# A gated product and its splits moved between two ticks, with tables, gates and small copies moved in their queues

## The chip, the cores and the metric

The kernel runs on one core of a Trainium2 chip. The core has several engines that each work through a queue of their own, in order: TensorE (PE, matrix products, results to PSUM banks), VectorE (DVE), ScalarE (ACT, functions from tables that have to be loaded), GpSimd (POOL), and SyncE (SP), which here issues the DMAs. Semaphores tie the queues together. The metric is the device time of one execution in microseconds (us); less is better.

## The reference

A block with 2048 tokens of width 576 takes two branches and mixes them by a gate for each token.

```
g = sigmoid((x * gate_w).sum(-1, keepdims=True))
a = _A_ref(x, A_wq, A_wk, A_wv, A_wo, A_beta)     # attention in 4 segments of 512, 32 heads of 18
b = _B_ref(x, B_w_gate, B_w_up, B_w_down)         # silu(x @ w_gate) * (x @ w_up) @ w_down, 576 -> 4608 -> 576
return g * a + (1 - g) * b
```

Branch a handles each segment with softmax attention inside it, and adds a linear memory `M` (with its normalizer `z`) of all segments before:

```
p = _softmax(logits, axis=-1)
a_dot = jnp.einsum("bhqk,bhkd->bhqd", p, vs)
...
a_mem = num / den
o = g * a_mem + (1.0 - g) * a_dot
...
pk = phi(ks)
M = M + jnp.einsum("bhld,bhle->bhde", pk, vs)
z = z + jnp.einsum("bhld->bhd", pk)
```

## The kernel before

The program is one long order of instructions, written out in Python. The order of the code is the order of each engine's queue. It has four stretches.

**Projections** (about 5 to 234 us). For each segment s of 512 tokens, ten chains of Q and K (`qk`, L449; n counts them) and then a loop of V steps (`v_step`, L475). Between the chains `upd_gen` (L496) updates the memory: it transposes `ph` tiles on PE (L513, L516), copies them out of PSUM into `kt` (512 columns by ACT at L514, 64 by DVE at L517), and multiplies them (L505). `mem_step` reads the memory (L550). Beside it all, inputs for the next stretch are made: sums on POOL (`rest_sum`, `first_sum`) and splits into a high half on ACT and a low one on DVE (`rest_split`, `first_split`). Tables by n say when: RSTEP (L661; a number j is a split, a negative one a sum), FSUM and FSPLIT (L729, L730).

**Half 0 and half 1 of the FFN** (to about 921 and 1631 us). The hidden width is cut into 36 slices, f = 0 to 35, and the tokens into two halves. For each half and f a block runs: seven products in the manner of Strassen (`seven`, L1421, j = 0 to 6) give the up and the gate values of two banks of 512 tokens. At the end ACT makes the silu `sg0` (L1540) and `sg1` (L1542), and DVE multiplies them by the up values: `sg0` from PSUM at L1548, after `seven(xx, 6)`, and `sg1` from SBUF at L1549. Each product is then split in fp16: high part `hh` on ACT (L1295), low part `hl` on DVE (L1298). `split_by(k, ...)` puts them on the list `due`, k ticks ahead; `lag` is the distance between the two.

Between the products a block has eight places named `tick()` (k = 0 to 7). Ticks 5 and 6 stand between `seven(y, 5)` and `seven(xx, 6)`, tick 7 behind it. Each tick runs what is due (weight preparation `w_make`, with L369 on POOL, L373 on ACT and L377 on DVE; splits; loads), and then, as `SHARE = (0, 0, 2, 2, 3, 3, 3, 3)` says, some of the **down groups**, with steps of attention between them (`att_gen`: scores L889 and L1002, exponentials on ACT L1006, maxima on DVE L907, probabilities by DVE L1102 and POOL L1106).

A down group multiplies three slices of `hh` and `hl` by the down weights `dw`: nine matmuls (L1162) into a bank, which DVE then adds to `ya` (L1171; L1169 for the first). `feed` (L1325) lists sixteen groups, eight token tiles by two column halves. They run in each block with q = f mod 3 = 0 and f > 0, for the three slices before it; groups 0 and 1 at tick 2, and so on to 7 to 9 at tick 5, 10 to 12 at tick 6 and 13 to 15 at tick 7. Two banks take turns, so that group n+2 waits for the eviction of group n.

The down weights of half 0 are split into three parts by `d_split` (L1139, L1140, L1142 or L1144). The gate of each token needs exponentials (`gates`, L1412 on). As silu and exponential have different tables on ACT, `exp_table` (L1418) runs a dummy exponential, so that the table is loaded at a chosen place.

**The break** after f = 35 of half 0 (about 899 to 921 us): the last sixteen down groups, ten beats in a row, without `seven` between them. The inputs of half 1's remainder products are split by `rest_second`, by a list `todo` with due times.

**The output** (1631 us to the end): the last down groups and the output projection.

Of the kernel before, what the change touches and what calls it, by code (L numbers as in the profile page):

```python
# [17 lines left out]
AF = mybir.ActivationFunctionType  # L18
OP = mybir.AluOpType
# [50 lines left out]
def gated_mix(ctx, tc, xT, xrest, wf, wfr, wfh, wd, wv, wo, beta, cmask, ident, bmask, out):  # L70
# [323 lines left out]
    with ExitStack() as st:  # L394
# [40 lines left out]
        def flush(keep=0):  # L435
            while len(late) > keep:
                z = late.pop(0)
                for d in z if isinstance(z, list) else [z]:
                    nc.sync.dma_start(*d)
# [56 lines left out]
        def upd_gen(s):  # L496
            acc = [pair_tile([P, 3, MW]), pair_tile([P, 2, MW])]
            Mo, Mn = Mm[s % 2], Mm[(s + 1) % 2]
            for i in range(5):
                if i:  # L500
                    for k in range(NT):
                        a, b = HR[k]
                        n = (b - a) * E
                        kk = P if k < 4 else 64
                        nc.tensor.matmul(acc[k // 3][:kk, k % 3, :n], kt[:, P * k:P * k + kk],  # L505
                                         vf[:, i - 1].rearrange("p h e -> p (h e)")[:, a * E:b * E],
                                         start=(i == 1 and k % 3 == 0), stop=(i == 4), skip_group_check=True)
                if i < 4:
                    kt = sp.tile([P, D], F32, name="kt", bufs=1)
                    c = slice(P * i, P * i + P)  # L510
                    ta = half_tile([P, 4, P])
                    for k in range(4):
                        nc.tensor.transpose(ta[:, k], phi[s, k, 1][:, c], idt)  # L513
                    nc.scalar.activation(kt[:, 0:512], ta.rearrange("p a b -> p (a b)"), AF.Copy)  # L514
                    tb = lone_tile([P, P])
                    nc.tensor.transpose(tb, phi[s, 4, 0][:, c], idt)  # L516
                    nc.vector.tensor_copy(kt[:, 512:576], tb[:, 64:128])  # L517
                yield
            for k in range(NT):
                n = (HR[k][1] - HR[k][0]) * E  # L520
                kk = P if k < 4 else 64
                t = acc[k // 3][:kk, k % 3, :n]
                if s == 0:
                    nc.vector.tensor_mul(Mn[:kk, k, :n], t, bm[:kk, k, :n])
                else:
                    tmp = sp.tile([P, MW], F32, name="mtmp")
                    nc.vector.tensor_mul(tmp[:kk, :n], t, bm[:kk, k, :n])
                    nc.gpsimd.tensor_add(Mn[:kk, k, :n], Mo[:kk, k, :n], tmp[:kk, :n])
            yield
# [128 lines left out]
            rest_16(XR[j], rr[((0, 0), (0, 0), (1, 1), (0, 1), (1, 0), (1, 1), (0, 1))[j]])  # L658

        XR = [None] * 7  # L660
        RSTEP = {2: (0, 3), 3: (5, -1), 4: (1, -4), 5: (4, -2), 6: (2,), 7: (-6,), 8: (6,)}  # L661
        rb, rs = {}, {}

        def b_load(i):
# [56 lines left out]
        def scan_load(t):  # L721
# [3 lines left out]
            if t in (21, 30):  # L725
                b_load(t // 30)

        blocks = {3: [(0, 0)], 4: [(0, 1)], 5: [(0, 2), (1, 0)], 6: [(1, 1)], 7: [(1, 2)]}
        FSUM = {3: [(1, 0), (4, 0)], 4: [(2, 0), (1, 1)], 6: [(4, 1), (2, 1)], 7: [(6, 0)], 8: [(6, 1)]}  # L729
        FSPLIT = {2: [(0, 0)], 3: [(5, 0), (0, 1)], 4: [(1, 0), (4, 0)], 5: [(5, 1), (2, 0)], 6: [(1, 1), (3, 0)],  # L730
                  7: [(3, 1), (4, 1)], 8: [(2, 1)]}
        for s in range(NSEG):
            upd = upd_gen(s - 1) if s else None
            casts = []
            for n, (m, u) in enumerate(chains):
                mid = []
                if s == 0:
                    for z in loads.get(n, []):
                        z()
                    if n + 3 < 9:  # L740
                        mid.append(lambda n=n: q_split(*chains[n + 3]))
                    if n in halves:
                        mid.append(lambda n=n: v_split(*halves[n]))
                if s == 1 and n < 3:
                    cast = masks(*((0, 3), (3, NT), (0, 0))[n])
                    casts.append(cast)
                if s == 1 and 3 <= n < 6:
                    mid.append(casts[n - 3])
                if (s, n) == (1, 7):
                    mid.append(betas)  # L750
                mid += scan_step(17 * s + n)
                if (s, n) == (1, 7):
                    mid.append(lambda: total(sx, 0, 20))
                if s == 2:
                    if n == 5:
                        mid.append(lambda: weigh(1, half_tile([P, 9])))
                    if n == 0:
                        rest_load()
                    for z in blocks.get(n, ()):
                        mid.append(lambda z=z: b_step(*z))  # L760
                    for j in RSTEP.get(n, ()):
                        mid.append(lambda j=j: rest_split(j) if j >= 0 else rest_sum(-j))
                if s == 3:
                    if n < 4:
                        first_load(n)
                    for j, z in FSPLIT.get(n, []):
                        if j in (0, 3, 5):
                            mid.append(lambda j=j, z=z: first_split(j, z))
                    for j, z in FSUM.get(n, []):
                        mid.append(lambda j=j, z=z: first_sum(j, z))  # L770
                    for j, z in FSPLIT.get(n, []):
                        if j in (1, 2, 4):
                            mid.append(lambda j=j, z=z: first_split(j, z))
                if s < 3:
                    for kt in ((0, 1), (2, 3), (4,))[n - 6] if s == 0 and n > 5 else (n - 4,) if s and n > 3 else ():
                        raws["x", kt] = x_load(s + 1, kt)
                qk(s, m, u, mid)
                flush(2)
                scan_load(17 * s + n)
                if upd is not None and n > 0:  # L780
                    next(upd, None)
# [16 lines left out]
            for n in range(8):  # L798
# [23 lines left out]
                else:  # L822
                    if n == 4:
                        wraw_of[1] = [w_load(1, u) for u in range(2)]
                    if n < 2:
                        first_split(6, n)
                    for k, t, v in ((0, rhs[0][96:], 0.0), (1, kst[0], -1.0), (3, kst[1], -1.0), (4, rhs[1][96:], 0.0)):
                        if n == k:
                            nc.gpsimd.memset(t, v)
# [13 lines left out]
    with ExitStack() as st:  # L843
# [479 lines left out]
                        c_open()  # L1323

        def feed(half, f):  # L1325
            return [(f // CH, i, hf, hs, ds, half) for i in range(8) for hf in range(2)]

        def x_second(new, z):
            r = {}
# [40 lines left out]
        def rest_second(rest):  # L1370
# [19 lines left out]
            def low(j):  # L1390
                t = rest[j][32:64]
                nc.vector.scalar_tensor_tensor(t, source(j)[32:64], sx[32:64], t, op0=OP.mult, op1=OP.subtract)

            todo = [(-1, load, 0), (0, high, 0), (0, high, 3), (1, low, 0), (1, low, 3), (4, load, 1), (11, high, 5),
                    (11, total, 1), (12, low, 5), (12, high, 1), (13, total, 4), (13, low, 1), (14, total, 2),
                    (14, high, 4), (15, low, 4), (15, total, 6), (16, high, 2), (16, low, 2), (17, high, 6), (18, low, 6)]
            return [(o, lambda fn=fn, j=j: fn(j)) for o, fn, j in todo]

        def glance(i, k):
# [12 lines left out]
        def gates():  # L1412
            nc.scalar.activation(gg, gl, AF.Exp, scale=-1.0)
            defer(2, lambda: nc.vector.tensor_scalar_add(gg, gg, 1.0))
            defer(3, lambda: nc.vector.reciprocal(gg, gg))
            defer(4, lambda: nc.vector.tensor_scalar(g1, gg, -1.0, 1.0, op0=OP.mult, op1=OP.add))

        def exp_table():  # L1418
            nc.scalar.activation(bg[:, 0:1], idt[:, 0:1], AF.Exp)
# [14 lines left out]
        for pos, (half, f) in enumerate(seq):  # L1434
# [49 lines left out]
            def tick():  # L1484
# [5 lines left out]
                if half == 0:  # L1490
# [6 lines left out]
                        d_scale(f // CH)  # L1497
                    if (f, k) == (2, 7) or (f > 2 and (q, k) == (1, 3)):
                        d_back(f // CH)
                    if f == 2 and k > 4 or f > 2 and (q, k) in ((1, 1), (1, 7), (2, 5 + int(f < FT - 1))):  # L1500
                        g = k - 5 if f == 2 else f - 1 if k == 1 else f
                        ds[half, g] = d_split(g, draw.pop(g))
                elif (q, k) in ((1, 0), (1, 2), (2, 1)):
                    g = f - 1 if k == 0 else f
# [12 lines left out]
            p5, sg0, sg1 = (row_tile() for _ in range(3))  # L1517
            seven(a, 0)
            nc.scalar.activation(xx, a, AF.Copy)
            if half == 0 and q == 0 and f:  # L1520
                exp_table()
                if f == CH:
                    gates()
            tick()
            seven(y, 1)
            nc.scalar.activation(p5, y, AF.Copy)
# [13 lines left out]
            nc.scalar.activation(sg0, sg0, AF.Silu, scale=iw[f // 4])  # L1540
            seven(y, 5, False)
            nc.scalar.activation(sg1, y, AF.Silu, scale=iw[f // 4])  # L1542
            if (half or q == 0) and not cps:
                exp_table()
            tick()
            tick()
            seven(xx, 6, False)
            nc.vector.scalar_tensor_tensor(sg0, xx, hk[f // 4], sg0, op0=OP.mult, op1=OP.mult)  # L1548
            nc.vector.scalar_tensor_tensor(sg1, p5, hk[f // 4], sg1, op0=OP.mult, op1=OP.mult)  # L1549
            split_by(2, hh[:, 0], hl[:, 0], sg0, int(q < CH - 1))  # L1550
            split_by(3, hh[:, 1], hl[:, 1], sg1)
            tick()
            assert not groups
            if f == FT - 1:
# [111 lines left out]
```

## Time and profile before

| | |
|---|---|
| three runs | 1721.46, 1718.13 and 1721.53 us, median 1721.46 |
| the profiled execution | 1718.78 us, of which the span from first to last instruction is 1717.1 |
| mean granted TensorE clock | 0.998 |
| projections | 0 to 234 us |
| half 0, break, half 1 | 234 to 899, 899 to 921, 921 to 1631 us |
| output | 1631 to 1717 us |

The profile gives for each engine its busy time, the chain of work that ended last, and groups of instructions by line, tile and form. `bank<-dw,hl` means that tile `bank` is written from `dw` and `hl`; `128x512 f16<-128x512 f32` are the shapes and types of output and input. Views of the trace give single instructions (start and duration in us), PE's waits by what ended them, and busy times in chosen windows. A matmul's row ends by a model of its pipeline, so rows of one engine may overlap a little.

### The profile page before, as it was taken

To read this page: it belongs to the slowest core of one execution; us is meant where nothing else is said; L and a number is where in the kernel's file an instruction comes from. 1 tells how busy PE (TensorE), PEld (TensorE's weight loads), DVE (VectorE), ACT (ScalarE), POOL (GpSimd) and SP (SyncE) were. 2 spreads that over 40 slices of the span, in tenths; PEclk is the share of its full clock that TensorE was granted. 3 is DMA by queue.
4 is the path that set the end of the run, shared out by engine and by line. 5 is a ranking of instruction groups with operands and counts; after the bars stand their busy time and mean duration, and the time that the engine had idled before them with its cause. 6 is when DMAs were issued, how large, how long until landed. Compare 5 with 4: busy or idle time off the path is not lost.

```text
span 1717.1 us, 35318 instructions
## 1 busy us (share of the span) xinstructions
PE 1679.5 (98%) x12269; PEld 1077.8 (63%) x12269; DVE 1353.8 (79%) x3295; ACT 1076.6 (63%) x1930; POOL 889.2 (52%) x1191
## 2 busy tenths in 40 slices
PE   9999999999999999999999999999999999999999
PEld 7898865556655665565555656556656656655577
DVE  6687676789888988898886878788878788776466
ACT  7666567777777777767774654665556566565411
POOL 3336562266667665665452665465546565554121
PEclk9999999999999999999999999999999999999999
DMA  8666675666776675446535486796696597574544
GB/s 282 218 232 222 214 260 208 208 200 177 231 223 208 168 244 192 154 121 195 169 123 164 114 192 158 163 219 136 147 215 166 121 221 167 140 163 125 156 157 145
DMA packets 349542, 314.25 MB, mean 183 GB/s; under 512 B 201268, under 2 KB 266548, under 8 KB 349364
## 3 DMA queue, kind: packets, MB, share of 16 engines
q1 hardware_dynamic: 349364, 312.00, 63.5%
q8 instruction: 96, 1.57, 0.4%
q14 instruction: 82, 0.67, 0.1%
HBM read 186.15 MB, written 99.55 MB: 166 GB/s over the span
## 4 chain that ended last, share of the span: by engine, by line
PE 73%; DVE 12%; ACT 7%; issue 3%; DMA 3%; POOL 1%; SPq 1%; DVEq 0%; ACTq 0%; POOLq 0%
PE bank L1426 31%; PE bank L1162 18%; PE bank L223 8%; PE bank L1429 5%; PE bank L889 3%; PE bank L1002 2%; DVE ya L1171 1%; PE bank L1030 1%; ACT L1540 1%; DVE junk L907 1%; PE bank L1032 1%; PE bank L964 1%; DVE p L1102 1%; ACT row L1540 1%; DMA rc<-rt 1%
## 5 line engine op out<-in xcount | busy, mean ns | idle before, releaser
L1162 PE MATMUL bank<-dw,hh 128*128 128x320 f16 (+1 forms) x2304 | 437.5, 286 | 13.3 <-DVE ya L1171 8.9
L1162 PE MATMUL bank<-dw,hl 128*128 128x320 f16 (+1 forms) x1152 | 330.1, 287 | 3.8 <-DVE hl L1298 3.2
L1106 POOL TENSOR_TENSOR p<-pe,p 128x512 f16<-128x512 f32 x220 | 271.9, 1236 | 75.3 <-DVE p L1102 50.6
L1162 PEld LDWEIGHTS <-hh 128*128 128x128 f16 x2304 | 225.3, 98 | 99.9 <-issue 18.1
L1006 ACT ACTIVATE pe<-bank 128x512 f32<-128x512 f32 x220 | 130.1, 592 | 183.6 <-PE bank L1002 167.5
L1171 DVE SCALAR_TENSOR_TENSOR ya<-bank,sc,ya 128x320 f32<-128x320 f32 x352 | 176.2, 511 | 55.0 <-PE bank L1162 53.3
L1429 PE MATMUL bank<-xr,rh 128*128 128x512 f16 x504 | 191.0, 379 | 0.0
L907 DVE CUSTOM_DVE_ANT_0 junk<-bank,cm 128x128 bf16<-128x128 f32 (+2 forms) x352 | 169.3, 481 | 13.7 <-PE bank L889 7.3
L1298 DVE SCALAR_TENSOR_TENSOR hl<-hh,row 128x512 f16<-128x512 f16 x144 | 129.7, 902 | 45.7 <-ACT hh L1295 44.8
L1014 POOL TENSOR_SCALAR_AFFINE_SELECT pe<-pe 128x256 f32<-128x256 f32 (+1 forms) x220 | 89.3, 406 | 144.9 <-ACT pe L1006 137.3
L1162 PEld LDWEIGHTS <-hl 128*128 128x128 f16 x1152 | 112.7, 98 | 34.3 <-DVE hl L1298 3.8
L889 PE MATMUL bank<-kst,qst 108*128 108x512 bf16 (+3 forms) x512 | 124.5, 299 | 3.6 <-ACT pe L1006 2.9
L1002 PE MATMUL bank<-qst,kst 111*128 111x512 bf16 (+3 forms) x352 | 103.2, 300 | 1.1 <-DVE acc L975 1.1
L1102 DVE CAST p<-pe 128x512 f16<-128x512 f32 x203 | 103.3, 510 | 0.0
L369 POOL TENSOR_TENSOR ws<-raw 128x256 f32<-128x256 f32 x72 | 65.6, 912 | 63.4 <-DMA raw<-in_wf_dram 32.2
L1538 DVE TENSOR_TENSOR row<-bank,row 128x512 f32<-128x512 f32 x72 | 49.6, 689 | 60.9 <-ACT bank L1537 60.8
L223 PE MATMUL bank<-xo,qhi 128*128 128x512 f32 x288 | 92.5, 401 | 1.3 <-ACT xo L132 0.7
L466 POOL TENSOR_TENSOR q<-qr,q 128x512 bf16<-128x512 f32 x36 | 47.8, 1329 | 84.8 <-ACT q L465 77.0
L1295 ACT ACTIVATE hh<-row 128x512 f16<-128x512 f32 x144 | 89.0, 618 | 3.7 <-DVE row L1548 3.0
L1533 ACT ACTIVATE row<-bank 128x512 f32<-128x512 f32 x72 | 42.9, 596 | 73.7 <-PE bank L1429 73.7
L1537 ACT ACTIVATE bank<-bank 128x512 f32<-128x512 f32 x72 | 41.9, 581 | 72.8 <-PE bank L1429 70.9
L1429 PEld LDWEIGHTS <-rh 128*128 128x128 f16 x504 | 49.3, 98 | 59.6 <-issue 0.2
(1102 smaller groups left out, 4213.9 us busy)
## 6 DMA issues: line engine op xcount, KB each, us to landing
xo<-in_wf_dram SPq DMA_DIRECT2D x65, 320.0 KB
raw<-in_wf_dram SPq DMA_DIRECT2D x72, 256.0 KB
dc<-dw SPq DMA_DIRECT2D x36, 432.0 KB
dw<-dc SPq DMA_DIRECT2D x36, 432.0 KB
rh<-rc SPq DMA_DIRECT2D x72, 168.0 KB
draw<-in_wd_dram SPq DMA_DIRECT2D x36, 288.0 KB
xo<-in_xT_dram SPq DMA_DIRECT2D x33, 256.0 KB
vd<-vps SPq DMA_DIRECT2D x8, 912.0 KB
```

The source lines that it names most:

```text
L223: nc.tensor.matmul(t, st[n], mv[n], start=(n == 0), stop=(n == 13))
L889: nc.tensor.matmul(t[:, c:c + w], qs[:KR, pr, P * i:P * i + P], ks[:KR, pr, 0:w], start=True, stop=True)
L907: nc.vector.tensor_tensor_reduce(junk.bitcast(BF)[:, :w], t[:, c:c + w], cm[:, L - w:L], 1.0, -3.0e38, OP.add, OP.max, m[:, k:k + 1])
L1002: nc.tensor.matmul(t[:, c:c + w], ks[:KR + 3, pr, P * j:P * j + P], qs[:KR + 3, pr, P * j:L], start=True, stop=True)
L1006: nc.scalar.activation(pe, t, AF.Exp, scale=SCALE)
L1102: nc.vector.tensor_copy(p1, pe)
L1106: nc.gpsimd.tensor_sub(p2, pe, p1)
L1162: nc.tensor.matmul(t, p, d[:, q, cs], start=(f == CH * c and n == 0), stop=(f == CH * c + CH - 1 and n == 2))
L1171: nc.vector.scalar_tensor_tensor(ya[:, i, cs], t, inv[c], ya[:, i, cs], op0=OP.mult, op1=OP.add)
L1298: nc.vector.scalar_tensor_tensor(lo, hi, -STEP, src, op0=OP.mult, op1=OP.add)
L1426: nc.tensor.matmul(t, w[:, p, z], x[z][:, q], start=first and n == 0, stop=False, skip_group_check=True)
L1429: nc.tensor.matmul(t, rem[:, RPOS[j]], XR[j], start=False, stop=True, skip_group_check=True)
```

## The change

- The 64-wide key copy of L517 is done by ACT.
- In segment 2 the last remainder sum is made one step earlier (n = 6), and its split behind chain (2, 8). In segment 3 what stood at n = 8 goes into the V loop.
- `exp_table` isn't called at f = 0, and at f = 3 only after `seven(y, 5)`, with `gates` behind it; from f = 6 on as before.
- The product of `sg1` (L1549) no longer stands behind that of `sg0`. In blocks with q = 0, other than the first of all, it stands between ticks 5 and 6, else between tick 6 and `seven(xx, 6)`.
- The splits change places: bank 1 (`sg1`) first, with the shorter lag, then bank 0. `feed` lists token tiles 4 to 7, which lie in bank 1, ahead of 0 to 3.
- The last down weight of half 0 is split at tick 2 in place of 5.
- The due times of `rest_second` from 11 on are two later.

```diff
-                    nc.vector.tensor_copy(kt[:, 512:576], tb[:, 64:128])
+                    nc.scalar.activation(kt[:, 512:576], tb[:, 64:128], AF.Copy)
...
-        RSTEP = {2: (0, 3), 3: (5, -1), 4: (1, -4), 5: (4, -2), 6: (2,), 7: (-6,), 8: (6,)}
+        RSTEP = {2: (0, 3), 3: (5, -1), 4: (1, -4), 5: (4, -2), 6: (2, -6)}
...
-        FSUM = {3: [(1, 0), (4, 0)], 4: [(2, 0), (1, 1)], 6: [(4, 1), (2, 1)], 7: [(6, 0)], 8: [(6, 1)]}
+        FSUM = {3: [(1, 0), (4, 0)], 4: [(2, 0), (1, 1)], 6: [(4, 1), (2, 1)], 7: [(6, 0)]}
...
-                  7: [(3, 1), (4, 1)], 8: [(2, 1)]}
+                  7: [(3, 1), (4, 1)]}
...
                 qk(s, m, u, mid)
+                if (s, n) == (2, 8):
+                    rest_split(6)
...
-                    if n < 2:
-                        first_split(6, n)
+                    if n == 0:
+                        first_split(2, 1)
+                        first_sum(6, 1)
+                    if 1 <= n < 3:
+                        first_split(6, n - 1)
...
         def feed(half, f):
-            return [(f // CH, i, hf, hs, ds, half) for i in range(8) for hf in range(2)]
+            return [(f // CH, i, hf, hs, ds, half) for i in (4, 5, 6, 7, 0, 1, 2, 3) for hf in range(2)]
...
-            todo = [(-1, load, 0), (0, high, 0), (0, high, 3), (1, low, 0), (1, low, 3), (4, load, 1), (11, high, 5),
+            todo = [(-1, load, 0), (0, high, 0), (0, high, 3), (1, low, 0), (1, low, 3), (4, load, 1), (13, high, 5),
...
-                    if f == 2 and k > 4 or f > 2 and (q, k) in ((1, 1), (1, 7), (2, 5 + int(f < FT - 1))):
-                        g = k - 5 if f == 2 else f - 1 if k == 1 else f
+                    if f == 2 and k > 4 or f > 2 and (q, k) in ((1, 1), (1, 7), (2, 6 if f < FT - 1 else 2)):
+                        g = k - 5 if f == 2 else f - 1 if (q, k) == (1, 1) else f
...
-            if half == 0 and q == 0 and f:
+            if half == 0 and q == 0 and f > CH:
                 exp_table()
-                if f == CH:
-                    gates()
...
-            if (half or q == 0) and not cps:
+            if (half or q == 0 and f) and not cps:
                 exp_table()
+                if half == 0 and f == CH:
+                    gates()
             tick()
+            if q == 0 and pos:
+                nc.vector.scalar_tensor_tensor(sg1, p5, hk[f // 4], sg1, op0=OP.mult, op1=OP.mult)
             tick()
+            if q or not pos:
+                nc.vector.scalar_tensor_tensor(sg1, p5, hk[f // 4], sg1, op0=OP.mult, op1=OP.mult)
             seven(xx, 6, False)
             nc.vector.scalar_tensor_tensor(sg0, xx, hk[f // 4], sg0, op0=OP.mult, op1=OP.mult)
-            nc.vector.scalar_tensor_tensor(sg1, p5, hk[f // 4], sg1, op0=OP.mult, op1=OP.mult)
-            split_by(2, hh[:, 0], hl[:, 0], sg0, int(q < CH - 1))
-            split_by(3, hh[:, 1], hl[:, 1], sg1)
+            split_by(2, hh[:, 1], hl[:, 1], sg1, int(q < CH - 1))
+            split_by(3, hh[:, 0], hl[:, 0], sg0)
             tick()
```

More of the change, by code (lines that the diff above doesn't have):

```diff
@@ L1392, in low @@
                 nc.vector.scalar_tensor_tensor(t, source(j)[32:64], sx[32:64], t, op0=OP.mult, op1=OP.subtract)
-            todo = [(-1, load, 0), (0, high, 0), (0, high, 3), (1, low, 0), (1, low, 3), (4, load, 1), (11, high, 5),
-                    (11, total, 1), (12, low, 5), (12, high, 1), (13, total, 4), (13, low, 1), (14, total, 2),
-                    (14, high, 4), (15, low, 4), (15, total, 6), (16, high, 2), (16, low, 2), (17, high, 6), (18, low, 6)]
+            todo = [(-1, load, 0), (0, high, 0), (0, high, 3), (1, low, 0), (1, low, 3), (4, load, 1), (13, high, 5),
+                    (13, total, 1), (14, low, 5), (14, high, 1), (15, total, 4), (15, low, 1), (16, total, 2),
+                    (16, high, 4), (17, low, 4), (17, total, 6), (18, high, 2), (18, low, 2), (19, high, 6), (20, low, 6)]
             return [(o, lambda fn=fn, j=j: fn(j)) for o, fn, j in todo]
```

## The prediction

> **What bounds the kernel now.** The page's first part, then its chain by engine, say that TensorE is the bound nearly everywhere.
>
> ```profile
> PE 1679.5 (98%) x12269; PEld 1077.8 (63%) x12269; DVE 1353.8 (79%) x3295; ACT 1076.6 (63%) x1930; POOL 889.2 (52%) x1191
> ```
>
> The change adds and removes no matmul. So only three things can move the end: the 37.6 us (1717.1 − 1679.5) in which PE stands still, the stretches in which its clock is lowered, and new waits. The list of PE's waits over the whole run (us in total, times, longest) says what the idle time hangs on:
>
> ```profile
> PE bank L1162 <- DVE ya L1171: 8.9, 18, 1.0
> PE bank L1162 <- DVE hl L1298: 3.2, 2, 2.1
> PE bank L505 <- DVE kt L517: 1.8, 2, 1.1
> PE bank L1426 <- ACT bank L1519: 1.7, 3, 0.6
> PE bank L550 <- DVE ph L468: 1.3, 1, 1.3
> PE bank L1162 <- DVE dw L1140: 1.1, 1, 1.1
> PE bank L1162 <- ACT hh L1295: 1.1, 2, 0.9
> PE bank L223 <- DVE r L486: 0.8, 1, 0.8
> PE bank L1162 <- DVE dw L1142: 0.6, 1, 0.6
> ```
>
> All but the first and the r row are waits that an edit aims at. The first, PE waiting for a PSUM bank that VectorE still evicts (`ya`), is the one that the change can lengthen. The table of windows shows the lowered clock (PEclk, third from the right), each time after a stretch in which PE was broken up:
>
> ```profile
> 273.00:276.60 3.60, 1.65 (x10) 0.71 (x9) 2.37 (x6) 3.26 (x8) 0.00 (x0) 1.00 0.90 304
> 277.10:280.60 3.50, 3.50 (x14) 1.73 (x12) 2.44 (x7) 1.41 (x3) 1.45 (x2) 0.53 1.03 393
> 898.90:903.90 5.00, 2.05 (x15) 1.16 (x13) 4.71 (x6) 2.80 (x6) 2.86 (x2) 1.00 0.13 47
> 905.10:908.60 3.50, 3.50 (x17) 2.30 (x16) 1.08 (x3) 0.00 (x0) 0.00 (x0) 0.52 0.94 284
> ```
>
> Half speed for 3.5 us costs about 1.7 us each time, 3.4 together.
>
> **The change part by part.** The timeline of PE gives each gap (start, duration, then idle time and releaser in brackets):
>
> ```profile
> 65.76 0.35 PE L505 MATMUL bank<-vf,kt 128*64 128x76 f32 x2 [1.06 <-DVE kt L517]
> 196.41 0.35 PE L505 MATMUL bank<-vf,kt 128*64 128x76 f32 x2 [0.72 <-DVE kt L517]
> 159.82 0.93 PE L550 MATMUL bank<-Mm,ph 128*128 128x152 f32 x6 [1.35 <-DVE ph L468]
> 248.53 1.46 PE L1426 MATMUL bank<-xo,wo__2849 128*128 128x512 f16 x6 [0.53 <-ACT bank L1519]
> 901.39 0.45 PE L1162 MATMUL bank<-dw,hh 128*128 128x320 f16 x2 [0.89 <-ACT hh L1295]
> 903.90 0.31 PE L1162 MATMUL bank<-dw,hl 128*128 128x320 f16 x1 [2.06 <-DVE hl L1298]
> 904.05 0.38 PE L1162 MATMUL bank<-dw,hh 128*128 128x256 f16 x2
> 1634.70 0.31 PE L1162 MATMUL bank<-dw,hl 128*128 128x320 f16 x1 [1.10 <-DVE hl L1298]
> ```
>
> A matmul's row is longer than its step in flow: 0.31 us at 903.90, but the next starts 0.15 later. So each gap loses some 0.16 more than its idle figure.
>
> *Key copies* (L517 from DVE to ACT, 12 times). Two gaps, 1.06 + 0.72 + 2 × 0.16 = 2.1. On ACT the copy follows L514 directly. No row shows a 64-wide one there; the 128x1 activation of L1419 takes 0.20 us (row below) and the 512-wide L514 takes 0.58, so it costs 0.20 to 0.58; I take 0.3, nearest the narrow one. ACT's timeline has L514 done well ahead of the first gap's end (start, duration):
>
> ```profile
> 62.76 0.58 ACT L514 ACTIVATE kt<-bank 128x512 f32<-128x512 f32 x1
> ```
>
> That is 63.34, over a microsecond ahead of PE's need, which hides the copy. Gain 2.0 (1.5 to 2.1).
>
> *Remainder sums*. In segment 2 the last sum moves a step earlier, where POOL is idle for 3.07 us:
>
> ```profile
> 150.72 1.39 POOL L466 TENSOR_TENSOR q<-qr,q 128x512 bf16<-128x512 f32 x1 [3.07 <-ACT q L465]
> ```
>
> So the long DVE subtraction which it stretched, and the split queued ahead of `ph`, leave the path. The gap is 1.35 + 0.16; the matmuls after it would wait about 0.4 for their own operand. Gain 1.1 (0.8 to 1.5). In segment 3 the r gap hangs on copies that aren't moved, and one more split stands at n=2: +0.1 (0 to 0.3).
>
> *Tables and gates*. Four table loads and two dummy exponentials go. Rows of ACT's timeline, and of its groups:
>
> ```profile
> 245.88 1.28 ACT L1419 ACT_TABLE_LOAD   x1
> 271.50 1.28 ACT L1419 ACT_TABLE_LOAD   x1
> L514 ACT ACTIVATE kt<-bank 128x512 f32<-128x512 f32 x12 | 6.9, 578 | 0.0
> L1419 ACT ACTIVATE bg<-idt 128x1 f32<-128x1 f32 x58 | 11.8, 203 | 0.6
> ```
>
> Most of ACT's 4 × 1.28 us is beside PE's work. On the path are the gap at 248.53 (0.53 + 0.16) and two smaller ones at 257.9 and 262.9, some 0.45 together: gain 1.15 (0.7 to 1.2). At f=3 the load and the two gate exponentials, 1.28 + 0.20 + 0.20, stand ahead of hh, and so of hl and the third weight's two splits, which are the dw waits of 1.1 and 0.6 in the list; with the two small waits beside them PE loses 2.45 there and, with everything on ACT 1.68 earlier, about 0.85 remains. Gain 1.6 (1.2 to 2.4). If that takes the lowered clock behind it away, 1.7 more (0 to 1.7).
>
> *Break after half 0*. The gaps at 901.39 and 903.90 lose 0.89 + 2.06 + 0.32 = 3.3. VectorE has six operations in a row there (4.71 us busy of 5.00), one of them this, ahead of the two hl that PE waits for (start, duration):
>
> ```profile
> 900.59 1.36 DVE L1549 SCALAR_TENSOR_TENSOR row<-row,sc 128x512 f32<-128x512 f32 x1
> ```
>
> The last weight's splits (0.8 and 1.4 us of DVE) move three ticks ahead and this product ahead of the last `seven`; bank 1, ready first, is then used first. PE needs the other bank only after eight groups. I leave 0.55 for the first hl: gain 2.75 (2.4 to 2.95), and the clock, 1.7 (0 to 1.7). The same order at the end of half 1 leaves a little of 1.10 + 0.16: gain 1.0 (0.4 to 1.26). The second half's remainder splits start two ticks later, where nothing on PE waits for them: 0.
>
> Sum of gains: 2.0 + 1.1 + 1.15 + 1.6 + 1.7 + 2.75 + 1.7 + 1.0 = **13.0** (7.0 to 15).
>
> *The price: the product of L1549 between ticks 5 and 6* in each block with down groups (q=0). There it is queued on VectorE ahead of the weight correction L377 and of the eviction of group 10, which frees the bank of group 12. Block f=18, from the timelines of DVE, POOL and PE:
>
> ```profile
> 580.16 0.38 DVE L1102 CAST p<-pe 128x512 f16<-128x512 f32 x1
> 580.46 0.74 DVE L377 SCALAR_TENSOR_TENSOR wo__7224<-ws,sc,wo__7224 128x512 f16<-128x512 f32 x1
> 581.12 0.54 DVE L1171 SCALAR_TENSOR_TENSOR ya<-bank,sc,ya 128x320 f32<-128x320 f32 x1
> 577.83 1.16 POOL L1106 TENSOR_TENSOR p<-pe,p 128x512 f16<-128x512 f32 x1
> ...
> 580.69 1.53 POOL L1106 TENSOR_TENSOR p<-pe,p 128x512 f16<-128x512 f32 x1 [1.34 <-PE bank L889]
> 581.72 0.43 PE L1162 MATMUL bank<-dw,hh 128*128 128x320 f16 x2
> ```
>
> VectorE, busy without a break, evicts group 10 only at 581.12 to 581.66, and PE's group 12 starts 0.06 later: no slack. The same step stands in all eleven such blocks of half 0 (0.05 or 0.06 between eviction and group 12). The product alone takes 0.74, start to start 0.66. That is the least that it costs here.
>
> It can cost more, by what POOL does. In the rows above, L1106 takes 1.53 us the second time, for 1.16 the first: it began 0.23 after L377 and stood still meanwhile. A second VectorE operation that follows then is held in turn, as the trace shows elsewhere (DVE, DVE, POOL):
>
> ```profile
> 647.98 0.77 DVE L377 SCALAR_TENSOR_TENSOR wo__8364<-ws,sc,wo__8364 128x512 f16<-128x512 f32 x1
> 648.74 1.58 DVE L1298 SCALAR_TENSOR_TENSOR hl<-hh,row 128x512 f16<-128x512 f16 x1
> 648.21 1.56 POOL L1106 TENSOR_TENSOR p<-pe,p 128x512 f16<-128x512 f32 x1
> ```
>
> Here L1298, 0.68 to 0.69 in rows with POOL idle, took 1.58 and ended 0.55 after POOL. After the change the product starts at 580.46 in L377's place, L1106 waits behind it as before and ends at 582.22, and L377 comes second: it ends at 582.22 + 0.55 = 582.77, not 581.20. Group 10 is evicted 1.58 later. In ten blocks (f=6 to 33) L1106 stands in this place, with 1.53 to 1.59 us: 10 × 1.58 = 15.8. At f=3 it doesn't: 0.66 + 0.17 for a gate operation, 0.8. The Trainium skill, "SBUF — State Buffer", section "Who interferes with whom", says that a VectorE instruction with two SBUF inputs and a GpSimd instruction that reads SBUF exclude each other through a shared port, and that issue order decides who blocks. The rows here agree.
>
> In half 1 the same place has slack in some blocks (0.2 to 1.7 us in five of eleven), L1106 starts after the product in most and before it in two: about 6 by the same reckoning. Against that the waits at tick 7 go, where L1549 stood ahead of an eviction beside POOL, such as
>
> ```profile
> 997.70 0.38 PE L1162 MATMUL bank<-dw,hh 128*128 128x256 f16 x2 [0.93 <-DVE ya L1169]
> L1549 DVE SCALAR_TENSOR_TENSOR row<-row,sc x72: 734/744/1648, 246.0 to 1632.1; 128x512 f32<-128x512 f32 x72
> ```
>
> (the second row: shortest, median and longest L1549; the longest is the one ahead of this gap). These sum to some 3.9, so half 1 nets +2.2 (−1 to +5). In half 0 nothing at tick 7 waits for an eviction, so nothing comes back. Blocks with q of 1 or 2 have no down groups between these places: 0.
>
> Sum of losses: 15.8 + 0.8 + 2.2 + 0.1 = **18.9** (6.6 + 3.1 = 9.7 to 24). Net: +5.9. From the profiled execution, 1718.78 us (its span is 1717.1), this gives 1724.7. The runs shown lie in two groups, 1718.1 and 1721.5, and the profiled one is in the lower; from the mean of the four, 1720.0, it is 1725.9, which I forecast.
>
> **The rivals.**
>
> *A, the product costs only itself.* Place: the q=0 blocks. If L1106 comes so late that L377 goes ahead of it, or its start slips with L1102's, each costs 0.66: losses 9.7, net −3.3, 1716.7. It decides the sign: with 13.0 − 3.1 = 9.9 us left over ten blocks, the change is faster where the eviction of group 10 is delayed by less than 0.99 us. For: 0.23 us between the two starts is little. Against: that interval is the same in nearly all ten blocks.
>
> *B, the product is covered.* If the order of attention's steps shifts so that group 12 no longer waits for that eviction, the ten cost nothing: net −10, 1710. Against it is the equal step in eleven of eleven blocks.
>
> *C, what the break and the clock should give doesn't come.* VectorE's operations there are moved, not removed; should another stand ahead of hl, and the lowered clock stay, 2.75 + 3.4 fall out: net +12, 1732. The Trainium skill, "TensorE: Matmul & The Clock Gate", Part 1, puts the drop down to an idle window of about 3.4 us. By that rule the drops would not hang on these gaps, whose longest is 2.06, and would stay; the trace has them only after them, so it speaks more for the gaps.
>
> *D, nothing to be seen*: an intermediate price, near 1.0 per block: 1720.
>
> **How the numbers follow.** Forecast 0.47, A 0.22, B 0.08, C 0.13, D 0.10. A measurement of this kernel can tell about 0.2%, 3.4 us, from no change. Faster: half of A, B, a little of D: 0.21. Same: the rest of A, most of D, the forecast's lower edge: 0.24. Slower: 0.55. The range reaches from A with the low group (1713) to C (1733); B and the ends of the tails are left out. The forecast's own range is 1721 to 1730.
>
> **What would show it.** The key copies right: no wait of L505 for the copy of L517's place. Tables: none loaded near 246 and 271, full clock at 277. Break: no gap over 1 us after 899, full clock behind it. The price: the list's row L1162 <- DVE ya rises from 8.9 to over 20 us, with gaps of about 1.6 us in ten blocks of half 0 and an L377 of some 1.6 us ahead of each; gaps of 0.7 with L377 at 0.74 would be A, none B. I am wrong above all if the order on VectorE isn't that of the code.

## The result and the profile after

The changed kernel took 1740.42 us in the median of four runs (1738.17 to 1741.75), the kernel before 1719.8 beside it (1717.06 to 1721.53). The ratio is 1.012, with an interval of 1.010 to 1.014: about 20 us slower, where 6 were forecast, with 1733 as the upper end. The direction and its cause were right and the size was not. The profiled execution of after took 1738.17 us, 19.4 more than that of before.

The list of PE's waits over the whole run of after (us in total, times, longest; lines are up to 9 higher than before, so L1167 is L1162, L1176 is L1171, L1174 is L1169, L1303 is L1298):

```profile
PE bank L1167 <- DVE ya L1176: 27.8, 22, 2.4
PE bank L1167 <- DVE ya L1174: 4.5, 3, 1.7
...
PE bank L1431 <- ACT bank L1524: 2.4, 4, 0.7
PE bank L223 <- DVE r L486: 2.0, 3, 0.8
...
PE bank L1167 <- DVE dw L1147: 0.6, 1, 0.6
...
PE bank L1167 <- DVE hl L1303: 0.2, 1, 0.2
```

The waits that the edits aimed at are gone or small: `kt` L517 isn't in the list, `hl` fell from 3.2 to 0.2. In their place the wait for VectorE's eviction of a down group rose from 8.9 to 27.8 us. Block f = 18 shows why, in the timelines of DVE, POOL and PE (start, duration):

```profile
585.35 0.39 DVE L1107 CAST p<-pe 128x512 f16<-128x512 f32 x1
585.64 0.75 DVE L1552 SCALAR_TENSOR_TENSOR row<-row,sc 128x512 f32<-128x512 f32 x1
586.31 1.65 DVE L377 SCALAR_TENSOR_TENSOR wo__7222<-ws,sc,wo__7222 128x512 f16<-128x512 f32 x1
587.87 0.54 DVE L1176 SCALAR_TENSOR_TENSOR ya<-bank,sc,ya 128x320 f32<-128x320 f32 x1
```

```profile
585.88 1.52 POOL L1111 TENSOR_TENSOR p<-pe,p 128x512 f16<-128x512 f32 x1 [1.34 <-PE bank L894]
```

```profile
588.47 0.43 PE L1167 MATMUL bank<-dw,hh 128*128 128x320 f16 x2 [1.58 <-DVE ya L1176]
```

The moved product (L1552) runs in 0.75, GpSimd's L1111 begins during it, and the weight correction L377 behind both takes 1.65 us, where it took 0.74. It ends 0.56 after GpSimd. The eviction (L1176) starts 1.56 later than it would, and so does PE.

Where the rest went: both traces have the same 12269 matmuls, of the same shapes in the same order, so the n-th start of one can be set against the n-th of the other. The sum of the steps between them, by stretch, against the terms of the prediction:

| stretch | forecast, us | measured, us |
|---|---|---|
| projections (to 234) | −3.0 | −2.4 |
| f = 0 to 3, up to its tick 6 (234 to 290) | −4.5 | −0.9 |
| tick 6 of f = 3 | +0.8 | +0.7 |
| tick 6 of ten blocks, f = 6 to 33 | +15.8 | +15.4 |
| lowered clock behind two of these | 0 | +3.3 |
| the rest of half 0 | 0 | +4.3 |
| the break | −4.5 | −4.6 |
| half 1 | +2.2 | +4.9 |
| end of half 1 | −1.0 | −1.3 |
| sum | +5.9 | +19.4 |

### The profile page after: what moved, and what is told of

The parts are those of the page before. It is cut to its first block, busy times and chain, and to the rows that moved or that the text cites. A ratio compares the mean times of both kernels' runs of the same rounds, so it can differ in the third digit from the quotient of the medians.

```text
span 1736.5 us, 35287 instructions
## 1 busy us (share of the span) xinstructions
PE 1683.3 (97%) x12269; PEld 1078.2 (62%) x12269; DVE 1359.8 (78%) x3283; ACT 1074.8 (62%) x1936; POOL 886.7 (51%) x1191
## 3 DMA queue, kind: packets, MB, share of 16 engines
q8 instruction: 96, 1.57, 0.4%
## 4 chain that ended last, share of the span: by engine, by line
PE 72%; DVE 12%; ACT 8%; issue 3%; DMA 3%; SPq 1%; POOL 1%; ACTq 0%; DVEq 0%; POOLq 0%
PE bank L1431 29%; PE bank L1167 19%; PE bank L223 9%; PE bank L1434 5%; PE bank L894 3%; PE bank L1007 2%; PE bank L1035 1%; DVE ya L1176 1%; ACT L1543 1%; DVE junk L912 1%; ACT row L1543 1%; DVE row L1552 1%; ACT L1424 1%; PE bank L969 1%; PE bank L1037 1%
## 5 line engine op out<-in xcount | busy, mean ns | idle before, releaser
L1167 PE MATMUL bank<-dw,hh 128*128 128x320 f16 (+1 forms) x2304 | 436.7, 286 | 32.5 <-DVE ya L1176 27.8
L1167 PE MATMUL bank<-dw,hl 128*128 128x320 f16 (+1 forms) x1152 | 330.1, 287 | 0.9 <-DVE dw L1147 0.6
L1111 POOL TENSOR_TENSOR p<-pe,p 128x512 f16<-128x512 f32 x220 | 271.7, 1235 | 79.5 <-DVE p L1107 49.4
L1167 PEld LDWEIGHTS <-hh 128*128 128x128 f16 x2304 | 225.2, 98 | 119.1 <-issue 39.2
L1176 DVE SCALAR_TENSOR_TENSOR ya<-bank,sc,ya 128x320 f32<-128x320 f32 x352 | 177.4, 511 | 63.1 <-PE bank L1167 61.0
L1303 DVE SCALAR_TENSOR_TENSOR hl<-hh,row 128x512 f16<-128x512 f16 x144 | 133.0, 924 | 48.4 <-ACT hh L1300 48.2
L1167 PEld LDWEIGHTS <-hl 128*128 128x128 f16 x1152 | 112.5, 98 | 31.9 <-DVE hl L1303 2.9
L1524 ACT ACTIVATE bank<-bank 128x512 f32<-128x512 f32 x72 | 41.9, 582 | 75.4 <-PE bank L1434 63.0
L1540 ACT ACTIVATE bank<-bank 128x512 f32<-128x512 f32 x72 | 41.9, 581 | 72.2 <-PE bank L1434 70.3
```

The lines of the kernel that those rows point to most:

```text
L1111: nc.gpsimd.tensor_sub(p2, pe, p1)
L1167: nc.tensor.matmul(t, p, d[:, q, cs], start=(f == CH * c and n == 0), stop=(f == CH * c + CH - 1 and n == 2))
L1176: nc.vector.scalar_tensor_tensor(ya[:, i, cs], t, inv[c], ya[:, i, cs], op0=OP.mult, op1=OP.add)
L1303: nc.vector.scalar_tensor_tensor(lo, hi, -STEP, src, op0=OP.mult, op1=OP.add)
```

## The experiments

Each ratio is to the kernel before, on the same chip.

**behind_tick6.** The product goes behind tick 6 in all blocks.

```diff
             tick()
-            if q == 0 and pos:
-                nc.vector.scalar_tensor_tensor(sg1, p5, hk[f // 4], sg1, op0=OP.mult, op1=OP.mult)
             tick()
-            if q or not pos:
-                nc.vector.scalar_tensor_tensor(sg1, p5, hk[f // 4], sg1, op0=OP.mult, op1=OP.mult)
+            nc.vector.scalar_tensor_tensor(sg1, p5, hk[f // 4], sg1, op0=OP.mult, op1=OP.mult)
```

> The changed kernel, but the product of sg1 stands between tick 6 and seven(xx, 6) in all blocks, also in those with q = 0. Theory: of the 20.6 us lost, the delay of group 10's eviction at tick 6 of half 0 is 15.6 + 0.7, the lowered clock behind two of these gaps 3.1, and the same place in half 1 some 6; all of this goes, while the q = 0 blocks now pay, as q = 1 and 2 do, about 1.4 for the copy that waits for the delayed product of sg0. 1740.4 - 25.4 + 1.4 gives about 1716. Rival (the tick-6 waits only show a lateness that other edits cause): above 1730.

Measured: 1719.18 against 1718.83, ratio 1.0009 (0.9998 to 1.002). By the ratios, the place between ticks 5 and 6 in q = 0 blocks costs some 19 us; without it the change is not clear of the kernel before. No lowered clock was left in its trace. It stayed 3 us above the estimate: half 0 still lost 5.4 us between 290 and 898 us.

**last_only.** Product, splits and feed order are those of before, except in the last block of each half.

```diff
-            if q == 0 and pos:
+            if f == FT - 1:
...
             nc.vector.scalar_tensor_tensor(sg0, xx, hk[f // 4], sg0, op0=OP.mult, op1=OP.mult)
-            split_by(2, hh[:, 1], hl[:, 1], sg1, int(q < CH - 1))
-            split_by(3, hh[:, 0], hl[:, 0], sg0)
+            if f == FT - 1:
+                split_by(2, hh[:, 1], hl[:, 1], sg1, int(q < CH - 1))
+                split_by(3, hh[:, 0], hl[:, 0], sg0)
+            else:
+                nc.vector.scalar_tensor_tensor(sg1, p5, hk[f // 4], sg1, op0=OP.mult, op1=OP.mult)
+                split_by(2, hh[:, 0], hl[:, 0], sg0, int(q < CH - 1))
+                split_by(3, hh[:, 1], hl[:, 1], sg1)
```

> The changed kernel, but product, splits and feed order are those of before in all blocks other than f = 35 of each half. Theory: the tick-6 price (19.4), the price in q = 1 and 2 (about 4) and half 1's loss (about 5) go, and all gains stay: 1740.4 - 28 = about 1712, faster than before by 7 or 8. Rival (the gains of tables and copies are given back anyway, or the break needs the order of all blocks): 1717 or more.

Measured: 1711.01 against 1718.83, ratio 0.9959 (0.9945 to 0.9973). The gains are there, and nearly all losses of after come from the order of the product and of what goes with it in the other 70 blocks. Segment 3's loss stays in this kernel (see last_s3).

**move_only.** The kernel before, with the product between ticks 5 and 6 in q = 0 blocks and nothing else.

```diff
             tick()
+            if q == 0 and pos:
+                nc.vector.scalar_tensor_tensor(sg1, p5, hk[f // 4], sg1, op0=OP.mult, op1=OP.mult)
             tick()
...
-            nc.vector.scalar_tensor_tensor(sg1, p5, hk[f // 4], sg1, op0=OP.mult, op1=OP.mult)
+            if q or not pos:
+                nc.vector.scalar_tensor_tensor(sg1, p5, hk[f // 4], sg1, op0=OP.mult, op1=OP.mult)
```

> The kernel before with one edit: in q = 0 blocks the product of sg1 stands between ticks 5 and 6. Theory: ten blocks at 1.56, one at 0.66, half 1 net 2 to 5, and 0 to 3 for a lowered clock behind the wider gaps: 1719.8 + 16.3 + 2 to 8 = 1738 to 1744; PE's waits for ya in half 0 rise from 6 to over 20 us. Rival (the price needs the other edits, by their phase): below 1730.

Measured: 1738.49 against 1718.83, ratio 1.012 (1.0104 to 1.0136), as expected. PE's waits between 290 and 890 us, of before and of this kernel:

```profile
PE bank L1162 <- DVE ya L1171: 4.8, 8, 1.0
```

```profile
PE bank L1162 <- DVE ya L1171: 19.5, 13, 2.4
```

In nine of the ten blocks the step is 1.50 to 1.56, in one 1.40. Three lowered stretches of the clock lie behind such gaps, and a fourth behind the break, which this kernel leaves as it was. The windows of one of the three:

```profile
707.00:710.00 3.00, 0.84 (x7) 0.45 (x6) 3.00 (x5) 0.43 (x1) 3.00 (x4) 0.97 0.09 32
710.00:713.00 3.00, 3.00 (x11) 1.49 (x10) 2.22 (x7) 0.54 (x2) 0.91 (x1) 0.50 0.21 64
```

**in_tick5.** The product goes into tick 5, ahead of its last attention step.

```diff
                 if groups and n < share:
                     down_groups(1)
+                if k == 5 and n == 2 and hook:
+                    hook.pop()()
...
+            if q == 0 and pos:
+                hook.append(lambda: nc.vector.scalar_tensor_tensor(sg1, p5, hk[f // 4], sg1, op0=OP.mult, op1=OP.mult))
             tick()
-            if q == 0 and pos:
-                nc.vector.scalar_tensor_tensor(sg1, p5, hk[f // 4], sg1, op0=OP.mult, op1=OP.mult)
```

> The changed kernel, but in q = 0 blocks the product of sg1 is queued inside tick 5, ahead of its last attention step, and no longer directly ahead of the weight correction L377. Theory (the product costs 0.66 itself, and 0.9 more because GpSimd's L1106 gets between it and L377): gaps ahead of group 12 shrink from 1.6 to about 0.7 in ten blocks, L377 takes 0.74 again, no lowered clock: 1740.4 - 9 - 3 = about 1728. Rival (VectorE is simply full there, and the order within it doesn't matter): 1740 within 2.

Measured: 1732.45 against 1718.83, ratio 1.008 (1.0065 to 1.0094). It lies between the two theories. PE's steps at group 12 shrank further than expected: to 3.9 us in the ten blocks (0.04 to 0.94), from 15.4. The timelines of f = 18, where the step is the largest, show what the first theory missed there (DVE, then POOL, then PE):

```profile
580.21 1.73 DVE L1555 SCALAR_TENSOR_TENSOR row<-row,sc 128x512 f32<-128x512 f32 x1
...
584.03 0.74 DVE L377 SCALAR_TENSOR_TENSOR wo__7222<-ws,sc,wo__7222 128x512 f16<-128x512 f32 x1
```

```profile
580.23 1.16 POOL L1111 TENSOR_TENSOR p<-pe,p 128x512 f16<-128x512 f32 x1
```

```profile
585.29 0.43 PE L1167 MATMUL bank<-dw,hh 128*128 128x320 f16 x2 [0.96 <-DVE ya L1176]
```

L377 is back at 0.74, as expected. But here the product itself meets GpSimd's L1111 and takes 1.73. So VectorE loses as much as in after, only earlier, where part of it is made up: PE's step at group 12 is 0.94, not 1.56. That the total still stayed above 1728 comes from elsewhere: a step of 1.53 ahead of an earlier group of f = 24, a lowered clock behind it, and half 1, which lost 7.1 us for the 4.9 of after. Why these came isn't shown.

**split_later.** The changed kernel, with the correction L377 of tick 6 moved to tick 7 in these blocks.

```diff
+            late = int(LEAD + o + 2 == 6 and f % CH == 1 and f > CH)
-            todo += [(LEAD + o, lambda k=k: high(k)), (LEAD + o + 2, lambda k=k: low(k)),
-                     (LEAD + o + 3, lambda k=k: keep(k))]
+            todo += [(LEAD + o, lambda k=k: high(k)), (LEAD + o + 2 + late, lambda k=k: low(k)),
+                     (LEAD + o + 3 + late, lambda k=k: keep(k))]
```

> The changed kernel, but the weight correction L377 that is due at tick 6 of q = 0 blocks from f = 6 on in half 0 runs at tick 7 (its store a tick later, too). So the product of sg1 takes L377's place ahead of group 10's eviction, instead of standing ahead of both. Theory (the price is the delay of that eviction by one more two-input operation that GpSimd holds up): the gaps of 1.6 ahead of group 12 fall to those of before, with them the lowered clock: 1740.4 - 15.6 - 3.1 = about 1722, if L377 costs nothing at tick 7. Rival (the product waits for its own inputs, or PE waits for another thing of that place): 1738 or more.

Measured: 1723.07 against 1717.35, ratio 1.003 (1.002 to 1.004). The product stays in its new place; with the second operation out of the way, the ten steps at group 12 are gone, PE's waits for the eviction between 290 and 890 us add up to those of before, and no clock is lowered:

```profile
PE bank L1168 <- DVE ya L1177: 4.9, 6, 1.9
```

Between f = 6 and 33 the price is therefore that of a second operation with two SBUF inputs ahead of the eviction, which GpSimd holds up, not of the product's own inputs.

**q12_only.** The kernel before, with the product ahead of `seven(xx, 6)` in blocks with q = 1 or 2.

```diff
             tick()
             tick()
+            if q:
+                nc.vector.scalar_tensor_tensor(sg1, p5, hk[f // 4], sg1, op0=OP.mult, op1=OP.mult)
             seven(xx, 6, False)
...
-            nc.vector.scalar_tensor_tensor(sg1, p5, hk[f // 4], sg1, op0=OP.mult, op1=OP.mult)
+            if not q:
+                nc.vector.scalar_tensor_tensor(sg1, p5, hk[f // 4], sg1, op0=OP.mult, op1=OP.mult)
```

> The kernel before with one edit: in blocks with q = 1 or 2 the product of sg1 stands ahead of seven(xx, 6) and so ahead of that of sg0. Theory: sg0's product, which frees the bank that ACT's first copy of the next block writes, waits behind the silu of sg1, and PE loses some 0.3 us per three slices and 0.7 in a few: 1718.8 + 4 to 5 = about 1723. Rival (as predicted, no cost there): 1719 within 1.5.

Measured: 1726.88 against 1717.35, ratio 1.0053 (1.0039 to 1.0066). This edit, costed at nothing in the prediction, costs 7 to 11 us. The theory had 4 to 5 for the whole. In its profiled execution half 0 lost 4.3 us by it (299 to 898 us), 4.1 of them ahead of L1426, matmuls of `seven`: 0.07 to 0.13 at the start of most blocks behind one with q = 1 or 2, and 0.4 to 0.7 at three, where the theory puts them. Half 1 lost 3.1 more, but only 0.5 of that ahead of L1426; the rest lies ahead of down groups and of attention's matmuls, in steps of at most 0.45. The mechanism of half 0 is seen best in the changed kernel at the end of f = 25, on DVE, ACT and PE:

```profile
726.92 1.24 DVE L1555 SCALAR_TENSOR_TENSOR row<-row,sc 128x512 f32<-128x512 f32 x1 [0.79 <-ACT row L1545]
728.09 0.74 DVE L1557 SCALAR_TENSOR_TENSOR row<-bank,sc,row 128x512 f32<-128x512 f32 x1
```

```profile
728.92 0.58 ACT L1524 ACTIVATE bank<-bank 128x512 f32<-128x512 f32 x1 [0.76 <-DVE row L1557]
```

```profile
729.55 0.81 PE L1431 MATMUL bank<-xo,wo__9340 128*128 128x512 f16 x3 [0.53 <-ACT bank L1524]
```

The product of `sg1` (L1555) waits for the second silu (L1545), which ACT makes after the first. The product of `sg0` (L1557) needs only the first silu and the bank, but is now second. It frees the bank that ACT's first copy of the next block (L1524) writes, and PE waits for that copy. q12_only has the same three steps there: the product of `sg0` at 720.57, the copy at 721.40 behind 0.75 of idle time, and PE at 722.03 behind 0.53. Before, on DVE and ACT at the same place:

```profile
715.58 0.75 DVE L1548 SCALAR_TENSOR_TENSOR row<-bank,sc,row 128x512 f32<-128x512 f32 x1 [0.22 <-ACT row L1540]
716.25 1.26 DVE L1549 SCALAR_TENSOR_TENSOR row<-row,sc 128x512 f32<-128x512 f32 x1
```

```profile
717.30 0.58 ACT L1519 ACTIVATE bank<-bank 128x512 f32<-128x512 f32 x1
```

**last_f3** and **last_s3.** Both start from last_only. The first moves ACT's squares of loaded weights (L140) a tick back at f = 3, the second restores segment 3's tables and loop.

```diff
-                    ((2, 2, 3, 4, 5, 6, 6, 7)[k], lambda: square(box[0], 20 + 9 * i + k))]
+                    ((2, 2, 3, 4, 5, 6, 6, 7)[k] + int(i == 2), lambda: square(box[0], 20 + 9 * i + k))]
```

```diff
-                    if n == 0:
-                        first_split(2, 1)
-                        first_sum(6, 1)
-                    if 1 <= n < 3:
-                        first_split(6, n - 1)
+                    if n < 2:
+                        first_split(6, n)
```

> The kernel of the run last_only, but ACT's squares of weights loaded for a bound (L140) come one tick later in block f = 3. Theory: what table and gates give at f = 3, and the lowered clock, is given back near 283 us, where ACT waits for these transfers ahead of its copy L1540, and so VectorE and PE wait (2.6 us): with the squares later that gap goes, 1711.0 - 2.5 = about 1708.5. Rival (PE there waits for something else, or for the next transfer): 1711 within 1.

> The kernel of the run last_only with segment 3's sums and splits where they stood before. Theory: the gap at 220 us (0.87) and that at 233 us (0.67) come from the sum put into the V loop, so they go: 1711.0 - 1.5 = about 1709.5. Rival (they have another cause): 1711.

Measured: 1710.74 and 1709.15 against 1717.35, ratios 0.9955 (0.9943 to 0.9968) and 0.9949 (0.9937 to 0.9962). Against last_only's 0.9959 neither is clear of the intervals; the traces say more. In last_only, ACT and PE at f = 3 (ACT waits 2.17 us for a transfer, and PE 2.45 for what comes of it):

```profile
280.75 0.74 ACT L140 ACTIVATE xo<-xo 128x640 f32<-128x640 f32 x1 [2.17 <-DMA xo<-in_wf_dram]
```

```profile
283.30 0.43 PE L1167 MATMUL bank<-dw,hh 128*128 128x320 f16 x2 [2.45 <-DVE ya L1174]
```

and PE in last_f3 at the same matmul, without a wait:

```profile
281.71 0.43 PE L1167 MATMUL bank<-dw,hh 128*128 128x320 f16 x2
```

The gap goes, as expected; but some 1.3 of the 2.6 us came back until f = 18, where PE's waits for another transfer, attention's keys, rose from 1.0 to 3.1 us. Segment 3's gap of 0.88 near 220 us went with the restored tables, and 0.5 of the 0.7 at 233 us. It came from the sum that the change puts on POOL beside a VectorE split, in after (DVE, POOL, PE):

```profile
218.45 1.68 DVE L137 SCALAR_TENSOR_TENSOR xo<-xo,sc,xo 128x512 f16<-128x512 f32 x1
220.05 0.45 DVE L486 TENSOR_TENSOR r<-bank,vps 128x288 f32<-128x288 f32 x1
```

```profile
218.29 1.29 POOL L631 TENSOR_TENSOR ph<-ph,xo 128x512 f32<-128x512 f32 x1
```

```profile
220.55 0.67 PE L223 MATMUL bank<-vw,xo 128*128 128x290 f32 x3 [0.67 <-DVE r L486]
```

**best** and **break_only.** The first has the edits of last_s3 and last_f3 together. The second is the kernel before with the edits for f = 35 alone.

```diff
-                    if f == 2 and k > 4 or f > 2 and (q, k) in ((1, 1), (1, 7), (2, 5 + int(f < FT - 1))):
+                    if f == 2 and k > 4 or f > 2 and (q, k) in ((1, 1), (1, 7), (2, 6 if f < FT - 1 else 2)):
...
+            if f == FT - 1:
+                nc.vector.scalar_tensor_tensor(sg1, p5, hk[f // 4], sg1, op0=OP.mult, op1=OP.mult)
             seven(xx, 6, False)
```

> The kernel of the run last_s3 with the later squares of last_f3. Theory: the two are independent, and what last_f3 wins at 283 us is mostly given back by transfers of attention's keys later: the same as last_s3 within 1 us, a ratio to before near 0.995. Rival (the two add up): ratio 0.993.

> The kernel before with the break's edits alone: early product, bank 1 first and feed order at f = 35 of both halves, the last down weight at tick 2, later remainder splits. Theory: the gap of 2.06 and most of that of 0.89 go (2.9), the lowered clock behind them (1.6) and the gap of 1.10 at the end of half 1 (1.2): 5.7 less than before, a ratio of 0.9967; the kernel last_only wins only some 2 us more by all other edits together. Rival (the lowered clock comes back elsewhere, or the break's waits move on): a ratio of 0.999.

Measured: 1707.29 and 1712.78 against 1717.42, ratios 0.9941 (0.9928 to 0.9954) and 0.9973 (0.996 to 0.9985). The best kernel of the study is 10 us faster than before and, by the ratios, some 31 faster than the change as it was made. Its interval overlaps that of last_s3, so what last_f3 adds isn't shown. The break alone gives about half: 5.8 us at the break and at the end of half 1 in its profiled execution, as expected.

## Why the prediction was right and wrong

**The price at tick 6 was right, in size and mechanism.** It said 1.58 us in ten blocks, an L377 of some 1.6 us and a wait list of over 20 us; after shows 1.54 to 1.57 in nine of them and 1.33 in one, 1.65 and 27.8. Rivals A, 0.66 per block, B, nothing, and D, near 1.0, were not the case. The break (4.5 forecast, 4.6 measured), the key copies (2.0 and 1.9) and the end of half 1 came as forecast, so rival C fell too.

**The step that failed most is the sentence "Blocks with q of 1 or 2 have no down groups between these places: 0".** It looked only at what is queued behind the product at ticks 5 to 7. What is queued behind it there is the product of `sg0`, whose bank the next block needs. q12_only shows 7 to 11 us for it. Half 0's rest (+4.3) is of this size and kind. Half 1's excess (4.9 for 2.2) is of this size, too: move_only, which moves the product in q = 0 blocks alone, lost 2.9 there, near the 2.2, and q12_only 3.1. But which wait carries it in half 1 isn't shown. The question "what is queued behind the waiting instruction, and who waits for that" had been put to one of the two places only.

**The clock behind the new gaps was costed at nothing.** The prediction counted two lowered stretches as gains, but none behind the ten gaps of 1.6 us and more that it foresaw. In after there are two, 3.3 us, in move_only three. The windows of after before, in and behind the first of them:

```profile
763.00:768.40 5.40, 3.05 (x49) 2.25 (x46) 5.30 (x10) 1.11 (x2) 4.47 (x6) 0.98 0.18 61
768.40:771.30 2.90, 2.90 (x12) 1.54 (x11) 1.95 (x5) 0.15 (x1) 1.04 (x1) 0.50 0.23 77
771.30:774.00 2.70, 2.70 (x19) 1.67 (x18) 1.46 (x5) 1.06 (x2) 1.53 (x2) 0.95 0.19 55
```

**The gains up to f = 3 were too large: 0.9 for 4.5 us.** The waits that were aimed at went: the "gain 1.6" at f = 3 came by 272 us, and no clock was lowered behind it. But both terms supposed that nothing else was late. A transfer was, for ACT's L140, and at 283.92 PE lost 1.86 of the time saved. Another 0.67 in this stretch, at 233.75, is the tail of segment 3's sum (below). The clock at 277 us wasn't a steady cost either. In break_only, move_only and q12_only this stretch is coded as before, and the clock stayed full. The windows of before, then of break_only, cut where the clock's steps of 3.41 us lie in each (see the last section):

```profile
273.59:277.00 3.41, 1.46 (x10) 0.65 (x8) 2.77 (x6) 2.67 (x7) 0.00 (x0) 1.00 0.89 318
277.00:280.41 3.41, 3.41 (x13) 1.70 (x12) 2.54 (x7) 1.22 (x3) 1.45 (x2) 0.50 1.03 393
```

```profile
274.48:277.89 3.41, 1.99 (x14) 1.36 (x14) 3.41 (x10) 1.99 (x5) 1.67 (x2) 1.00 1.04 375
277.89:281.30 3.41, 3.41 (x26) 2.29 (x24) 1.99 (x6) 2.79 (x8) 0.12 (x1) 1.00 1.03 384
```

So a part of the term was read off one execution in which it happened to occur. The lowered clock behind the break is another matter: it came in all three traces that are coded as before there (before, move_only, q12_only).

**Segment 3's moved sum** was costed at 0.1 and took 0.9 at 220 us and 0.7 at 233.75: the prediction asked what the split costs and not what POOL's sum does to a VectorE operation beside it, though it had used just that in segment 2.

What stays open: half 1's steps in q12_only, what held in_tick5 above its estimate, and how much of the ±2 us between executions is due to transfers in the blocks from f = 3 to f = 20.

## What to carry to other kernels

An operation moved within a full queue is priced by what stands behind it until the next thing that the bound engine waits for, and that question has to be put at every place where it lands, the harmless-looking ones too. Two VectorE operations with two SBUF inputs in a row cost more than the sum of their rows where a GpSimd operation arrives during the first. Time saved ahead of a stretch that waits for transfers can be given back there, and a lowered clock seen in one execution is no steady cost until a second shows it.

## What the runs showed of the hardware

**VectorE and GpSimd take turns.** The same product took 0.75 us when GpSimd's L1111 came 0.24 after it, and 1.73 when it came with it at 580.2; L377 took 0.74 or 1.65 by the same rule. This agrees with the Trainium skill, "SBUF — State Buffer", section "Who interferes with whom": a VectorE instruction with two SBUF inputs contends with a GpSimd one that reads SBUF, and issue order decides who blocks. The rows add that the one kept waiting goes next, so a second VectorE operation in the queue doesn't pass it.

**The lowered clock lies on a grid of 3.41 us, and PE's work in one cell of the grid decides on the next.** By the clock's records in the traces, each lowered stretch behind a gap lasts 3.41 us, and those of one execution start a whole number of 3.413 us apart: in after at 768.17 and 829.61 (18 cells), in move_only at 354.84, 709.83, 829.30 and 924.87 (104, 35 and 28). Two neighbouring cells of after, and two more:

```profile
764.76:768.17 3.41, 1.45 (x14) 1.08 (x12) 3.41 (x6) 1.11 (x2) 2.87 (x3) 1.00 0.02 5
768.17:771.58 3.41, 3.41 (x14) 1.78 (x12) 2.46 (x8) 0.43 (x1) 1.27 (x2) 0.50 0.23 79
703.32:706.73 3.41, 2.54 (x48) 2.00 (x44) 3.20 (x12) 1.12 (x2) 2.28 (x3) 1.00 0.00 0
706.73:710.14 3.41, 2.12 (x15) 1.39 (x15) 3.41 (x8) 0.20 (x1) 2.84 (x4) 1.00 0.23 79
```

The gap of 1.96 us ahead of 767.89 lies within one cell, which leaves PE 1.45 us of work there, and the next cell ran at half clock. The gap of 2.16 ahead of 708.02 is longer, but a border at 706.73 cuts it: 2.54 and 2.12 us of work, and full clock. In move_only the same gap falls within one cell (706.42 to 709.83, 1.25 us of work), and the clock fell. Eleven of the twelve traces have a lowered stretch, some only at their very end, and so show where their grid lies. In them, leaving out the first and the last microseconds, every cell with up to 1.4 us of work was followed by a lowered one and none with 1.65 or more; from 1.45 to 1.60 both happened, and these figures rest on rows whose ends are modelled. As the grid lies elsewhere from execution to execution, the same code can lose this time in one and not in the next.

The Trainium skill, "TensorE: Matmul & The Clock Gate", Part 1, says that the window of the gate runs free, so that a change of clock depends on where in it the work falls; that fits these rows. It puts the drop down to at least one idle window of about 3.4 us; here a window with 1.45 us of work in it was enough.
